# Attention and FFN on one core: scores from parts for three more pairs of batch two, their normalising on GpSimd, new prices in the order's planner

## The chip, the cores and the metric

The kernel runs on one core of a Trainium2 chip. The metric is the device time in microseconds of one execution; lower is better.

## What is computed

Causal attention for 4 batches of 12 heads, 448 positions and 64 dimensions, then a layer norm and a two-layer FFN (768 to 3072 to 768) with a residual. All arrays are float32 to the caller.

```python
scores = scale * np.matmul(q, k.transpose(0, 1, 3, 2))      # causal mask, softmax over k
x = np.matmul(attn, v)                                      # heads side by side: 4 x 448 x 768
xn = (x - mu) / np.sqrt(var + 1e-06) * g_ln
out = x + np.maximum(xn @ w_ch1, 0.0) @ w_ch2
```

## The kernel before

**Tiles and stages.** Heads go in pairs, six to a batch; a pair fills the 128 partitions with two times 64 dimensions. Batches are counted from 0 here, so that "batch two" of the title is batch index 1. Batch 0's attention runs first; the attention of batch index 1 runs beside the FFN of batch index 0, and so on. The FFNs of batch indexes 2 and 3 run together at the end as a `Pair`, with seven products of halves in place of eight. FFN weights are split into two parts of type F32R, high and low, and an FFN matmul has three products (`wh xh`, `wh xl`, `wl xh`) of 448 columns each. Tiles named `ph`, `po`, `bX`, `bY`, `bA` are its results.

**Scores of a pair, two ways.** `both` (L868) takes q and k as loaded, in F32, and issues the matmuls of the two heads side by side, each on 64 of the array's rows (operand `first_qk` for batch 0, `qkraw` for batch index 1), in three groups of the four row blocks: `[3], [0, 2], [1]`. `scores` (L893) uses all 128 rows: `split1` and `split2` (L839, L848) first make `qs` (q above, its rounding rest below), `kh` and `kl` (the parts of k), and two matmuls of type F32R add up in one bank. `BOTH` (L66) names the batches that go by `both` beside batch 0. A row block i has 112 (i + 1) columns: 112, 224, 336, 448. `least` then masks and takes the running minimum on DVE, `exps` the exponential on ACT, `norm` (L934) multiplies each row block by the reciprocal sum: on GpSimd for batch 0, on DVE or ACT for the others. `transposes` (L963) turn the blocks on TensorE (results `pt`), `pv` (L986) multiplies by the values: eight matmuls on 64 columns each side, results `px`, 16 records in the profile. `TWOS` (L77) lists pairs whose value matmuls are issued together with the next pair's.

**Layer norm.** `mean` (L1041) sums over partitions with a matmul of ones; `squares` (L1069) ends with the column `ve` = 1/sigma; `spread` (L1094) and, for the last two batches, `banks` (L1239) turn it to rows with four transposes (`rb`), and `apply1` scales the input of the FFN.

**Order of the work.** Nothing is issued directly. `Plan` records every instruction as a task with the time by which it is needed, `cost` (L300) gives each a duration, and `run` (L419) goes through a list schedule of the five queues (TensorE, GpSimd, DVE, ACT and SP, which issues all DMAs). `t.mode` is TensorE's form: "" for the whole array, "rows" for matmuls on 64 rows, "columns" for those on 64 columns. A change of form costs `CHANGE` in the plan, and work of the present form goes first unless other work is due `TOGETHER` earlier (L486 to L492). Where `either` gives several engines for a task, the schedule chooses. `MOVES` shifts due times of some tasks by drawn amounts, `STARTS` gives the slots at which pairs start. The resulting order is fixed in the program; on the chip, semaphores do the waiting.

Of the kernel before, what the change touches and what calls it, by code (L numbers as in the profile page):

```python
# [11 lines left out]
F32 = mybir.dt.float32  # L12
# [11 lines left out]
P = 128  # L24
# [17 lines left out]
SECOND = 16000  # L42
BEHIND = 12000
EARLY_SLOT = 1450
SLACK, DMA_SLACK = 154, 5280
CHANGE, TOGETHER = {'': 0, 'columns': 100, 'rows': 188}, 13200
# [12 lines left out]
BOTH, RAT = (1,), [0, 0, 0]  # L59
SAT, TAT, NAT, END = [0, 0, 1, 1, 2], [4, 5, 5, 6, 6], [3, 3], 7  # L60
EV1, EV = [1, 1, 1, 1, 1], [1, 1, 0, 1, 0]
STARTS = {
    0: [-1, 6, 12, 18, 24, 30],
    1: [0, 5, 10, 14, 19, 24],
    2: [30, 34, 38, 42, 46, 50],
    3: [54, 58, 62, 66, 70, 74],  # L66
# [4 lines left out]
TWOS = {3: [0, 2, 4]}  # L71
VAR0, RB0, XC, XG = 1, 5, 3, 3
SPLIT = (1, 2, 3)
COPIED = [NP, NP, 3, 0]
AHEAD0 = 4
WARM, FILL, HOLD = 10, 29160, 4000
# [7 lines left out]
NDVE = 7  # L84
# [12 lines left out]
class View:  # L97
# [44 lines left out]
    def to_broadcast(self, shape):  # L142
        return self._new(self.p, self.idx, lambda t: t.to_broadcast(shape))

# [55 lines left out]
class Plan:  # L200
# [99 lines left out]
    def cost(self, t):  # L300
# [3 lines left out]
        if t.engine == "sync":  # L304
            x = (t.outs + t.ins)[0]
            rate = 360 if x.p[1] - x.p[0] == P else 240 if x.p[1] - x.p[0] == D else 150 if n == 512 else 330
            cost = 650 if x.buf.name == "first_qk" else 60
            return cost, (x.p[1] - x.p[0]) * n * 4 * 320 / rate, False
        if t.engine == "tensor":
            if t.kw.get("rhs") is not None and t.kw["rhs"].dtype == BF16:  # L310
                return 0.84 * n, 220, False
            if t.method == "transpose":
                return 97 if t.ins[0].dtype == F32 else 80, 220, False
# [93 lines left out]
    @staticmethod  # L407
    def drawn(n, seed):
# [10 lines left out]
    def run(self, need, hint):  # L419
# [9 lines left out]
        tiled = {"": [], "rows": [], "columns": []}  # L429
# [26 lines left out]
        while True:  # L456
# [28 lines left out]
            elif e == "tensor":  # L485
# [3 lines left out]
                heap = min((h for h in tiled.values() if h), key=lambda h: h[0])  # L489
                same = tiled[mode]  # L490
                if same and same[0][0] < heap[0][0] + TOGETHER:
                    heap = same  # L492
# [103 lines left out]
def kernel(ctx, tc, qk, v, w1, w2, g, out):  # L596
# [172 lines left out]
    class Att:  # L769
        count = {"nm": 0, "PT": 0}  # L770

        def __init__(self, b):
            self.b, self.twos = b, TWOS.get(b, [])
            self.t = {}
            self.turn = 0
            self.done = set()
# [35 lines left out]
        def load(self, p):  # L812
# [4 lines left out]
            elif self.b in BOTH:  # L817
# [8 lines left out]
        def load_v(self, p):  # L826
# [3 lines left out]
            else:  # L830
                pool = probs if p - 1 in self.twos else ap
                vt = pool.tile([C, 2, NC, D], F32, tag="v", name="vt", bufs=1)
# [101 lines left out]
        def norm(self, p, h):  # L934
# [6 lines left out]
            eng = nc.vector if self.b or p >= NDVE else nc.gpsimd  # L941
            for i in (0, 1, 3, 2):
# [4 lines left out]
                if eng is nc.gpsimd:  # L947
# [719 lines left out]
```

## Time and profile before

| | us |
|---|---|
| three runs | 792.99, 793.04, 793.08 |
| median | 793.04 |
| the profiled execution's own time | 792.73 |
| its span, first to last instruction | 790.7 |
| PE busy in the span | 783.6 |
| DVE, ACT, POOL busy | 665.8, 519.0, 303.0 |

The span is cut into pieces by engine and line. PE is TensorE's matmul row, PEld its weight load. Matmuls are pipelined, so the duration of one is longer than its distance to the next; distances are read from starts. The granted clock is 0.999 of full speed over the span, which is the level of 2.4 GHz. Every instruction that the plan issues carries the same line, L587, so work is told apart by tile names. The chain in order of time lists what released what, with runs of alike instructions as one piece; its pieces follow one another, so their lengths add up to the time.

### The profile page before, as it was taken

To read this page: it belongs to the slowest core of one execution; us is meant where nothing else is said; L and a number is where in the kernel's file an instruction comes from. 1 tells how busy PE (TensorE), PEld (TensorE's weight loads), DVE (VectorE), ACT (ScalarE), POOL (GpSimd) and SP (SyncE) were. 2 spreads that over 40 slices of the span, in tenths; PEclk is the share of its full clock that TensorE was granted. 3 is DMA by queue.
4 is the path that set the end of the run, shared out by engine and by line. 5 is a ranking of instruction groups with operands and counts; after the bars stand their busy time and mean duration, and the time that the engine had idled before them with its cause. 6 is when DMAs were issued, how large, how long until landed. Compare 5 with 4: busy or idle time off the path is not lost.

```text
span 790.7 us, 13663 instructions
## 1 busy us (share of the span) xinstructions
PE 783.6 (99%) x4554; PEld 720.0 (91%) x4554; DVE 665.8 (84%) x1406; ACT 519.0 (66%) x1155; POOL 303.0 (38%) x306
## 2 busy tenths in 40 slices
PE   9999999999999999999999999999999999999998
PEld 4679888888899989999898899999999999999998
DVE  6899998989999998888887479887887878888785
ACT  6999978888999775766755255664545546455461
POOL 4645000001262262242111168655546464464540
PEclk9999999999999999999999999999999999999999
DMA  9788889677778878778886765335253342523434
GB/s 212 269 255 289 319 308 349 209 295 249 303 250 310 303 277 286 249 270 278 249 311 204 251 193 173 112 92 168 62 161 102 107 130 78 157 90 115 126 94 167
DMA packets 62470, 166.50 MB, mean 211 GB/s; under 512 B 7136, under 2 KB 27744, under 8 KB 62400
## 3 DMA queue, kind: packets, MB, share of 16 engines
q1 hardware_dynamic: 62400, 165.63, 63.3%
q8 instruction: 36, 0.59, 0.3%
q14 instruction: 34, 0.28, 0.1%
HBM read 116.62 MB, written 39.94 MB: 198 GB/s over the span
## 4 chain that ended last, share of the span: by engine, by line
PE 92%; ACT 4%; DVE 2%; DMA 1%; issue 0%; POOL 0%; SPq 0%; ACTq 0%; POOLq 0%; DVEq 0%
PE po L587 21%; PE bX L587 21%; PE ph L587 18%; PE bY L587 10%; PE sc L587 6%; PE bA L587 5%; PE px L587 5%; PE pt L587 5%; ACT P L587 1%; ACT bits L587 1%; DVE P L587 0%; DMA scratch<-w 0%; DMA first_qk<-qk_dram 0%; DVE wl L587 0%; DVE w L587 0%; ACT wh L587 0%
## 5 line engine op out<-in xcount | busy, mean ns | idle before, releaser
L587 ACT ACTIVATE P<-P,least 112x336 f32<-112x336 f32 (+3 forms) x176 | 91.2, 522 | 26.4 <-DVE least L587 25.9
L587 PE MATMUL ph<-xh,wh 128*128 128x450 f32 (+1 forms) x288 | 104.4, 364 | 0.2 <-DVE hl L587 0.2
L587 PE MATMUL po<-hh,wh 128*128 128x448 f32 x288 | 103.9, 361 | 0.0
L587 PE MATMUL ph<-xh,wl 128*128 128x450 f32 (+1 forms) x288 | 102.8, 359 | 0.0
L587 PE MATMUL po<-hl,wh 128*128 128x448 f32 x288 | 102.8, 357 | 0.0
L587 PE MATMUL ph<-xl,wh 128*128 128x450 f32 (+1 forms) x288 | 102.8, 358 | 0.0
L587 PE MATMUL po<-hh,wl 128*128 128x448 f32 x288 | 102.5, 356 | 0.0
L587 ACT ACTIVATE wp<-s 128x256 fp32r<-128x256 f32 (+1 forms) x114 | 51.6, 461 | 58.1 <-PE bX L587 16.4
L587 DVE CUSTOM_DVE_ANT_0 P<-sc,mask 112x224 f32<-112x224 f32 (+3 forms) x176 | 71.5, 441 | 13.7 <-PE sc L587 12.2
L587 POOL TENSOR_TENSOR s<-u 128x256 f32<-128x256 f32 (+1 forms) x60 | 55.3, 937 | 68.2 <-DMA u<-scratch 48.7
L587 ACT ACTIVATE wk<-u 128x256 fp32r<-128x256 f32 (+1 forms) x89 | 41.1, 464 | 54.3 <-PE bX L587 36.1
L587 DVE TENSOR_TENSOR wp<-s,wp 128x256 fp32r<-128x256 f32 (+1 forms) x120 | 68.6, 582 | 3.1 <-ACT wp L587 2.8
L587 POOL TENSOR_TENSOR h<-b,h 128x448 fp32r<-128x448 f32 x36 | 43.2, 1201 | 52.5 <-ACT h L587 31.9
L587 POOL TENSOR_TENSOR kl<-qkraw,kh 128x896 fp32r<-128x896 f32 x12 | 28.7, 2392 | 86.8 <-ACT kh L587 42.7
L587 POOL TENSOR_TENSOR acc<-acc,xT 128x448 f32<-128x448 f32 x12 | 15.5, 1291 | 118.4 <-DVE xT L587 98.1
L587 ACT ACTIVATE PT<-pt 112x448 f32<-112x448 f32 x88 | 45.8, 540 | 22.7 <-PE pt L587 21.1
L587 PEld LDWEIGHTS ph<-xh,wh 128*128 128x128 f32 x288 | 54.4, 189 | 2.7 <-issue 1.7
L587 DVE TENSOR_TENSOR xT<-xT,bX 128x448 f32<-128x448 f32 x72 | 44.5, 618 | 14.3 <-PE bX L587 14.2
L587 PEld LDWEIGHTS ph<-xl,wh 128*128 128x128 f32 x288 | 54.5, 189 | 2.1 <-issue 1.7
L587 PEld LDWEIGHTS po<-hl,wh 128*128 128x128 f32 x288 | 54.6, 189 | 1.5 <-issue 1.1
L587 PEld LDWEIGHTS ph<-xh,wl 128*128 128x128 f32 x288 | 54.4, 189 | 1.5 <-DVE xl L587 0.5
L587 PEld LDWEIGHTS po<-hh,wl 128*128 128x128 f32 x288 | 54.5, 189 | 0.7 <-issue 0.5
(193 smaller groups left out, 2174.8 us busy)
## 6 DMA issues: line engine op xcount, KB each, us to landing
raw<-w_dram SPq DMA_DIRECT2D x39, 768.0 KB, 6.7
scratch<-w SPq DMA_DIRECT2D x48, 384.0 KB, 4.7
full<-scratch SPq DMA_DIRECT2D x24, 768.0 KB, 6.9
kept<-wl SPq DMA_DIRECT2D x30, 384.0 KB, 5.8
qkraw<-qk_dram SPq DMA_DIRECT2D x12, 896.0 KB, 5.5
u<-scratch SPq DMA_DIRECT2D x24, 384.0 KB, 3.8
u<-scratch SPq DMA_DIRECT2D x36, 256.0 KB, 2.9
PR<-P SPq DMA_DIRECT2D x18, 490.0 KB, 6.5
```

The lines of the kernel that those rows point to most:

```text
L587: getattr(getattr(nc, t.engine), method)(*args, **kw)
```

## The change

- `BOTH` becomes a list of pairs for each batch: of batch index 1, pairs 0, 1 and 2 stay with `both`; pairs 3, 4 and 5 go by `split1`, `split2` and `scores`.
- `NORMS` sets the engine of `norm` for each pair: P is GpSimd, E is DVE or ACT. Batch index 1's pairs 1 to 5 go to GpSimd.
- `TWOS` adds pair 4 of batch index 2, whose value matmuls are issued with pair 5's.
- `SENT`: 1/sigma of batch index 2 is written to a row in memory and read back broadcast, in place of four transposes. `WIDE`: in `spread` of batch index 1 the mean is copied to a PSUM bank.
- `mean` stores the two parts with even and odd elements apart and reads them woven, as the FFN does, and both matmuls depend on both parts.
- The last addition of the pair's FFN and its store are cut into two halves.
- In the planner: transposes have a form of their own ("turned"), prices of changes are 10, 178 and 192 ns, the preference for the present form is 70 times the price of the change, `SLACK`, `SECOND`, `HOLD`, `MOVES`, `SAT` and two `STARTS` have other values.

```diff
-SECOND = 16000
+SECOND = 32000
-SLACK, DMA_SLACK = 154, 5280
-CHANGE, TOGETHER = {'': 0, 'columns': 100, 'rows': 188}, 13200
+SLACK, DMA_SLACK = 192, 5280
+CHANGE, NEAR, TOGETHER = {'': 0, 'turned': 10, 'columns': 178, 'rows': 192}, 192, 70
...
 MOVES = [
-    (305651422, 1000, 256, 16860, 90000), (1865966318, 1000, 128, -20100, 79900),
-    (1507149061, 3000, 128, 242781, 302781), (1428196934, 3000, 32, 161652, 221652),
-    (690608532, 20000, 32, 389252, 399252), (1144641184, 8000, 16, 48048, 58048),
-    (637256214, 20000, 16, 259121, 279121), (1540864739, 8000, 16, 268427, 278427),
-    (635955765, 3000, 256, 110408, 120408),
+    (305651422, 1000, 256, 16860, 90000), (1507149061, 3000, 128, 242781, 302781),
+    (1428196934, 3000, 32, 161652, 221652), (637256214, 20000, 16, 259121, 279121),
+    (1073982846, 1000, 64, -6297, 53703), (475912916, 20000, 16, 212061, 232061),
+    (272716789, 1000, 32, 168281, 228281), (1922429363, 8000, 32, 353206, 363206),
 ]
...
-BOTH, RAT = (1,), [0, 0, 0]
-SAT, TAT, NAT, END = [0, 0, 1, 1, 2], [4, 5, 5, 6, 6], [3, 3], 7
+BOTH, RAT = {1: [0, 1, 2], 2: [], 3: []}, [0, 0, 0]
+SAT, TAT, NAT, END = [0, 0, 1, 0, 2], [4, 5, 5, 6, 6], [3, 3], 7
...
 STARTS = {
-    0: [-1, 6, 12, 18, 24, 30],
+    0: [-1, 6, 12, 17, 24, 30],
     1: [0, 5, 10, 14, 19, 24],
     2: [30, 34, 38, 42, 46, 50],
-    3: [54, 58, 62, 66, 70, 74],
+    3: [54, 58, 62, 67, 70, 74],
 }
...
-TWOS = {3: [0, 2, 4]}
+TWOS = {2: [4], 3: [0, 2, 4]}
...
-SPLIT = (1, 2, 3)
+SPLIT, SENT, WIDE = (1, 2, 3), (2,), ('mb',)
...
-WARM, FILL, HOLD = 10, 29160, 4000
+WARM, FILL, HOLD = 10, 29160, 3200
...
-NDVE = 7
+NORMS = ['PPPPPP', 'EPPPPP', 'EEEEEE', 'EEEEEE']
...
+
+    def turned(self, f):
+        return self._new(self.p, self.idx, f)
...
+            if x.buf.name.startswith("row"):
+                return 60, 1000 * 320, False
             return cost, (x.p[1] - x.p[0]) * n * 4 * 320 / rate, False
...
             if t.method == "transpose":
-                return 97 if t.ins[0].dtype == F32 else 80, 220, False
+                t.mode = "turned"
+                return 97 if t.ins[0].dtype == F32 else 78, 220, False
...
     @staticmethod
+    def changed(old, new):
+        if old == new:
+            return 0
+        return NEAR if {old, new} == {"rows", "columns"} else max(CHANGE[old], CHANGE[new])
+
...
-        tiled = {"": [], "rows": [], "columns": []}
+        tiled = {x: [] for x in CHANGE}
...
                 while heap:
                     x = heapq.heappop(heap)
                     heapq.heappush(tiled[tasks[x[1]].mode], x)
-                heap = min((h for h in tiled.values() if h), key=lambda h: h[0])
-                same = tiled[mode]
-                if same and same[0][0] < heap[0][0] + TOGETHER:
-                    heap = same
+                heap = min(
+                    (h[0][0] + TOGETHER * self.changed(mode, x), h[0][1], x) for x, h in tiled.items() if h
+                )
+                heap = tiled[heap[2]]
...
-            elif self.b in BOTH:
+            elif p in BOTH[self.b]:
...
-            eng = nc.vector if self.b or p >= NDVE else nc.gpsimd
+            way = NORMS[self.b][p]
             for i in (0, 1, 3, 2):
                 pp = self.t["P", p, h][:, OFF[i]:OFF[i + 1]]
                 kw = dict(
                     out=pp, in0=pp, scalar1=r[:, i // 3, i % 3:i % 3 + 1], scalar2=1.0, op0=ALU.mult, op1=ALU.mult,
                 )
-                if eng is nc.gpsimd:
-                    eng.tensor_scalar(**kw)
-                else:
-                    nc.either(
-                        ("vector", "tensor_scalar", (), kw),
-                        ("scalar", "activation", (), dict(
-                            out=pp, in_=pp, func=ACTF.Copy, scale=r[:, i // 3, i % 3:i % 3 + 1],
-                        )),
-                    )
+                ways = [
+                    ("gpsimd", "tensor_scalar", (), kw),
+                    ("vector", "tensor_scalar", (), kw),
+                    ("scalar", "activation", (), dict(
+                        out=pp, in_=pp, func=ACTF.Copy, scale=r[:, i // 3, i % 3:i % 3 + 1],
+                    )),
+                ]
+                nc.either(*[ways[x] for x in {"P": (0,), "E": (1, 2), "A": (0, 1, 2)}[way]])
 
...
             mb = ps.tile([P, S], F32, tag="sc", name="mb", bufs=2)
             if self.b in SPLIT:
                 hi, lo = (ap.tile([P, S], F32R, tag="PT", name="acc" + x, bufs=8) for x in "hl")
-                move(hi, self.acc)
-                lows = dict(out=lo, in0=self.acc, in1=hi.bitcast(F32), op=ALU.subtract)
+                move(halves(hi), apart(self.acc))
+                lows = dict(
+                    out=halves(lo), in0=apart(self.acc), in1=halves(hi).bitcast(F32), op=ALU.subtract
+                )
                 nc.either(("gpsimd", "tensor_tensor", (), lows), ("vector", "tensor_tensor", (), lows))
+                last = [n for n, w, _ in lo.buf.log if w]
                 for x, t in enumerate((hi, lo)):
-                    nc.tensor.matmul(mb, lhsT=ones.to_broadcast([P, P]), rhs=t, start=(x == 0), stop=(x == 1))
+                    nc.record("tensor", "matmul", (mb,), dict(
+                        lhsT=ones.to_broadcast([P, P]), rhs=woven(t), start=(x == 0), stop=(x == 1),
+                    )).deps.update(last)
             else:
                 nc.tensor.matmul(
                     mb, lhsT=ones.bitcast(F32).to_broadcast([P, P]), rhs=self.acc, start=True, stop=True
@@ -1086,13 +1109,28 @@
...
+            if self.b in SENT:
+                self.row = dr.tile([1, S], F32, name=f"row{self.b}")
+                nc.sync.dma_start(out=self.row.turned(lambda t: t.rearrange("o (i c) -> c (o i)", c=C)), in_=ve)
+
+        def sigma(self, tag, bufs):
+            t = ap.tile([P, S], F32, tag=tag, name="rbs", bufs=bufs)
+            nc.sync.dma_start(out=t, in_=self.row.turned(lambda t: t.broadcast_to([P, S])))
+            return t
 
         def over_sigma(self):
+            if self.b in SENT:
+                self.rb = self.sigma("rb", 1)
+                return
             self.rb = ap.tile([P, S], F32, tag="rb", name="rbs", bufs=1)
             move(self.rb, self.spread_one(self.t["ve"]))
 
         def spread(self):
-            self.t["mb"], self.t["rb"] = self.kept, self.spread_one(self.t["ve"])
+            self.t["mb"] = self.kept
+            self.t["rb"] = self.sigma("PT", 8) if self.b in SENT else self.spread_one(self.t["ve"])
+            for x in WIDE:
+                src, self.t[x] = self.t[x], ps.tile([P, S], F32, tag="sc", name=x, bufs=2)
+                move(self.t[x], src)
             self.parts()
             self.xg = [ap.tile([P, S], F32, tag="PT", name="xg", bufs=8) for _ in range(XG)]
...
-                if self.b and self.b not in BOTH:
+                both = self.b == 0 or p in BOTH[self.b]
+                if not both:
                     put(pre, t0 - (2 if self.b == 1 else 1), self.split1, p)
                     put(pre, t0 - 1, self.split2, p)
...
-                for x, grp in enumerate([] if self.b and self.b not in BOTH else RGROUPS if p or self.b else FIRSTS):
+                for x, grp in enumerate([] if not both else RGROUPS if p or self.b else FIRSTS):
...
-                for x, grp in enumerate(SGROUPS if self.b and self.b not in BOTH else []):
+                for x, grp in enumerate([] if both else SGROUPS):
                     put(post, t0 + sat[x], self.scores, p, grp)
...
             for a in self.at:
                 a.t["rb"] = rb = ps.tile([P, S], F32, tag="pt", name="rb", bufs=2)
-                for x in range(NC):
+                if a.b in SENT:
+                    move(rb, a.sigma("PT", 8))
+                for x in range(NC) if a.b not in SENT else ():
                     nc.tensor.transpose(
                         rb[:, x * C:(x + 1) * C], a.t["ve"][:, x:x + 1].to_broadcast([C, P]), ident[:C, :C]
                     )
...
             def add(i, j, src):
                 m = 2 * blk[2] + i
                 t = self.at[j].xT[m]
-                nc.vector.tensor_tensor(out=t, in0=t, in1=src, op=ALU.add)
                 self.left[j, m] -= 1
-                if self.left[j, m] == 0:
-                    nc.sync.dma_start(out=out[self.at[j].b, m], in_=t)
+                last = (b, k) == self.items[-1]
+                for x in ((0, S // 2), (S // 2, S)) if last else ((0, S),):
+                    y = slice(*x)
+                    nc.vector.tensor_tensor(out=t[:, y], in0=t[:, y], in1=src[:, y], op=ALU.add)
+                    if self.left[j, m] == 0:
+                        nc.sync.dma_start(out=out[self.at[j].b, m][:, y], in_=t[:, y])
```

## Rows read from the trace of the kernel before

**Rows 1.** Of the page: busy time of TensorE; shares of the chain that ended last.

```profile
PE 783.6 (99%) x4554; PEld 720.0 (91%) x4554; DVE 665.8 (84%) x1406; ACT 519.0 (66%) x1155; POOL 303.0 (38%) x306
...
PE 92%; ACT 4%; DVE 2%; DMA 1%; issue 0%; POOL 0%; SPq 0%; ACTq 0%; POOLq 0%; DVEq 0%
```

**Rows 2.** Busy time by stretch: start:end, us, then each engine's busy us (instructions), clock, DMA.

```profile
0.00:80.00 80.00, 76.71 (x491) 54.34 (x492) 67.57 (x206) 72.36 (x186) 41.85 (x74) 1.00 0.85 258
80.00:480.00 400.00, 399.76 (x2452) 361.64 (x2450) 348.18 (x765) 288.67 (x621) 103.08 (x71) 1.00 0.79 271
...
100.00:200.00 100.00, 100.00 (x599) 85.35 (x598) 91.11 (x211) 83.08 (x167) 6.72 (x5) 1.00 0.78 284
```

**Rows 3.** The chain in order of time, 136 to 146 us: start us, us, what.

```profile
136.65 0.94 PE sc L587 x4
137.59 2.09 PE po L587 x10
139.68 0.95 PE sc L587 x8
...
142.34 0.57 PE sc L587 x4
```

**Rows 4.** The chain in order of time, 183 to 192 us.

```profile
184.32 0.94 PE sc L587 x4
...
187.29 0.95 PE sc L587 x8
...
189.96 0.56 PE sc L587 x4
```

**Rows 5.** The chain in order of time, 291 to 303 us.

```profile
291.92 2.04 PE px L587 x16
293.95 5.30 PE ph L587 x27
299.26 0.86 PE sc L587 x6
300.12 1.13 PE ph L587 x6
301.25 0.39 PE sc L587 x4
...
301.85 0.38 PE sc L587 x2
```

**Rows 6.** The chain in order of time, near 268 us and 378 us.

```profile
268.64 0.38 PE rb L587 x4
269.03 1.15 PE po L587 x6
...
377.96 3.92 PE px L587 x32
```

**Rows 7.** Groups of DVE, 98 to 200 us; then tiles r, qs, kl: duration ns min/median/max.

```profile
L587 DVE TENSOR_SCALAR P<-P,r 112x448 f32<-112x448 f32 (+3 forms) x27 | 8.4, 363 | 0.1
...
L587 DVE TENSOR_SCALAR P<-P,r x88: 264/386/2418, 101.5 to 426.1; 112x448 f32<-112x448 f32 x26, 112x336 f32<-112x336 f32 x23, 112x224 f32<-112x224 f32 x20, 112x112 f32<-112x112 f32 x19
...
L587 POOL TENSOR_SCALAR P<-P,r x32: 357/498/642, 10.4 to 43.3; 112x112 f32<-112x112 f32 x8, 112x224 f32<-112x224 f32 x8, 112x448 f32<-112x448 f32 x8, 112x336 f32<-112x336 f32 x8
...
L587 DVE TENSOR_TENSOR qs<-qkraw,qs x12: 1089/2002/3058, 146.6 to 412.0; 64x896 fp32r<-64x896 f32 x12
...
L587 ACT ACTIVATE qs<-qkraw x10: 934/941/986, 144.7 to 408.4; 128x896 fp32r<-128x896 f32 x10
...
L587 POOL TENSOR_TENSOR kl<-qkraw,kh x12: 2135/2144/3271, 190.7 to 408.6; 128x896 fp32r<-128x896 f32 x12
```

**Rows 8.** Order of time from 786.5 us; DMA issues (KB each, us to landing); stores of out_dram.

```profile
787.14 0.62 DVE L587 TENSOR_TENSOR xT<-xT,bX 128x448 f32<-128x448 f32 x1 [0.51 <-PE bX L587]
...
wk<-kept SPq DMA_DIRECT2D x54, 128.0 KB, 2.1
...
DMA to landing us min/median/max: 1.9/2.6/10.7
```

More of the change, by code (lines that the diff above doesn't have):

```diff
@@ L407, in drawn @@
     @staticmethod
+    def changed(old, new):
+        if old == new:
+            return 0
+        return NEAR if {old, new} == {"rows", "columns"} else max(CHANGE[old], CHANGE[new])
+    @staticmethod
     def drawn(n, seed):
@@ L773, in __init__ @@
             self.b, self.twos = b, TWOS.get(b, [])
+            if b == 1 and self.twos:
+                self.more = ap.tile([P, 4 * S], F32, tag="qkraw", name="more", bufs=1)
             self.t = {}
@@ L831, in load_v @@
                 pool = probs if p - 1 in self.twos else ap
-                vt = pool.tile([C, 2, NC, D], F32, tag="v", name="vt", bufs=1)
+                if self.b == 1 and p - 1 in self.twos:
+                    vt = self.more[:C, 2 * S:2 * S + 2 * NC * D].rearrange("p (h j d) -> p h j d", h=2, j=NC)
+                else:
+                    vt = pool.tile([C, 2, NC, D], F32, tag="v", name="vt", bufs=1)
             nc.sync.dma_start(out=vt, in_=v[self.b, p])
@@ L968, in transposes @@
                 self.count["PT"] += 1
-            t = ap.tile([C, S], F32, tag=tag, name="PT", bufs=bufs)
+            if self.b == 1 and tag in ("y", "rb"):
+                t = self.more[:C, :S] if tag == "y" else self.more[:C, S:2 * S]
+            else:
+                t = ap.tile([C, S], F32, tag=tag, name="PT", bufs=bufs)
             o = 0
```

## The prediction

> **What bounds the kernel now.** I read the page first. Its busy table and its chain that ended last [rows 1] say that TensorE carries the program: PE is busy for 783.6 of 790.7 us and has 92% of the chain. A busy PE alone proves little, so I read the busy times by stretch next [rows 2]. From 80 to 480 us PE is busy for 399.76 of 400 us. Only the first 80 us have idle PE time, 3.29 us (80 less 76.71), beside the tail. In the stretch 100 to 200 us, where most of the edited work lies, DVE is busy for 91.11 us and ACT for 83.08, POOL for 6.72. Third I read the chain in order of time at the places that the diff touches [rows 3 to 6]. There the pieces follow each other on PE without a hole, so from 80 us on the time is the sum of PE's pieces, and an edit is worth what it takes from that sum. An FFN matmul counts 0.19 us (6 in 1.13 us) [rows 5].
>
> What this chain also shows is the price of a change of form. An FFN run behind a visit of score matmuls from 64 rows, or of value matmuls, is about 0.20 us longer than its count: 10 matmuls in 2.09 us instead of 1.89 [rows 3], 27 in 5.30 instead of 5.10 behind a value visit [rows 5]. So each visit that stands alone costs 0.20 us on top of its own pieces. Scores from parts don't show it: the six FFN matmuls behind them take the plain 1.13 us [rows 5].
>
> **The change part by part.**
>
> *Three pairs of batch two.* Pairs 3, 4 and 5 of batch index 1 are scored by `both` now. Pair 3 has visits of 0.94, 0.95 and 0.57 us, 2.46 us together, two of them alone (0.40 us) and the third beside a value visit [rows 3]: 2.86 us. Pair 5 has 0.94 and 0.95 on the two sides of a value visit, and 0.56 alone [rows 4]: 2.45 + 0.20 = 2.65 us. Pair 4 repeats pair 5's pattern. Sum 8.16 us. The value visit stays in both kernels and pays its own change. After the change a pair is scored as batch index 2 is: 0.86 us for a head's widths 448, 112 and 336, 0.39 us for width 224 of both heads, 0.38 for the other head's 448 [rows 5], and the other head's 112 and 336, which are 0.86 - 0.38 = 0.48. That is 2.11 us a pair, 6.33 for three. **Gain 1.8 us.** Its bounds: 1.0 if the value visits, which lose their neighbours, meet T or score visits badly (0.2 us at each of four places), 2.6 if they all find one another.
>
> Here a rule of the Trainium skill speaks against the edit. TensorEngine Tiling (Array Packing), section Theoretical Speedup, promises up to twice the speed where the contraction is 64 or less, and `both` is such a packing; leaving it should cost, and by the page the three pairs would go from 7.4 us of pieces to an estimated 14.8. The trace doesn't agree: 2.11 us against 2.45 before any change of form [rows 4, 5]. In the code the two parts are tiles of type F32R and the packed operands are F32, so the two forms are not alike but for the packing.
>
> *What feeds them.* Each of the three pairs now needs two moves, on ACT about 0.94 us each, a DVE subtraction (1.09 at the least, 2.00 at the median) and a POOL subtraction of 2.14 us [rows 7]. The load has twice the bytes of a pair's two small loads. On SP these stand in front of weight loads; the issue count falls by one a pair. All that lies beside PE. Its cover is ACT's 17 and DVE's 9 idle us of the stretch 100 to 200 [rows 2], and if it is gone scores come late and PE waits: the third rival.
>
> *Normalising on POOL.* In 98 to 200 us DVE gives 8.4 us to 27 such instructions [rows 7], which go, with ACT's share. POOL does one in 0.498 us at the median [rows 7], so a pair of 2 heads by 4 takes 4.0 us on an engine that has 93 us free. The wait that this adds is for POOL: transposes of a pair now wait behind its queue, where kl and the running sum stand too. A pair has some 24 us to the next one's start (pairs 3 and 5 start at 136.65 and 184.32 us) [rows 3, 4], so I cost it at nothing. Bounds: 1 us of gain in the early part, where batch index 1's pair 1 leaves ACT and DVE, and the loss of the third rival.
>
> *One more shared value visit.* A value visit alone takes 2.04 + 0.20 us [rows 5], two together 3.92 [rows 6] + 0.20. 4.48 - 4.12 = 0.36; I take **0.3**, since one of batch index 2's two last visits stood beside score pieces already and may lose a neighbour. Bounds 0 and 0.36.
>
> *Sigma of batch index 2 through memory.* Four transposes go: 0.38 us and 0.02 us of the run behind them (6 matmuls in 1.15 us instead of 1.13) [rows 6]. **Gain 0.4.** In their place stand two DMAs and one PSUM fill on ACT or DVE, with a whole batch's FFN between them and their reader; cover is ample. A load that the trace doesn't show, 4-byte pieces to a row, can take several times the 2.1 us of a plain small one [rows 8] before it matters. The copy of the mean to PSUM for batch index 1 is one ACT or DVE instruction, takes a second SBUF operand from six DVE instructions, and holds the second of the two score banks until the sixth is done; scores of batch index 2 queue behind that, PE goes on with FFN matmuls (six follow the rb transposes at once) [rows 6]: zero.
>
> *Prices of the plan.* Transposes get a mode with 10 ns a change. The row confirms the size: 0.02 us behind a visit [rows 6]. Bunching can save only that on each visit; I take **0.1**, bounds 0 and 0.6. The other prices hardly change a choice (13200 before, 12460 to 13440 now). New seeds and starts redraw the whole order; I take zero and carry +-1.6 us, half of PE's idle 3.29 us at the start [rows 2]. The woven mean takes the same two matmuls: zero, bounds +-0.3.
>
> *The tail.* The last addition ends at 787.14 + 0.62 = 787.76 us [rows 8], 2.94 us before the end of the span, and its store of 224 KB lands in 2.6 us. With halves, the second ends some 0.1 us later (a second fixed part) and moves 112 KB, near the 2.1 us of a 128 KB load [rows 8]. **Gain 0.2**, bounds +0.2 lost and 0.5 gained.
>
> Sum: 1.8 + 0.3 + 0.4 + 0.1 + 0.2 = 2.8 us. The profiled execution took 792.73 us, 0.31 under the median of 793.04. 792.73 - 2.8 = 789.9, and with 0.31 the forecast is **790.2 us**. A measurement of this kernel can tell about 0.2% from no change, which is 1.6 us: faster is below 791.4, slower above 794.6.
>
> **The rivals.**
>
> 1. *The start closes as well.* ACT is busy for 72.4 and DVE for 67.6 of the first 80 us, and PE idles there [rows 2]; with a pair's normalising gone to POOL, half or all of the 3.29 us can go. 790.2 - 1.6 = 788.6, at most 786.9. Against it: batch index 0 normalised on POOL before, so only one pair is relieved there.
>
> 2. *The gain is given back in small waits.* From 80 us on PE had 0.24 us of idle time in 400 [rows 2]; a redrawn order can hardly be better and can be worse. Each of the three pairs has a new late comer, kl on POOL, 2.14 us [rows 7] behind that engine's normalising. If each is late by 0.9 us, 2.7 us come back: 792.9 us. For it speaks that such a subtraction took up to 3.27 us [rows 7]; against it, that batch index 2 lives with the same chain and no idle PE.
>
> 3. *DVE becomes the bound in 100 to 200 us (slower).* POOL gets 4 pairs by 8 by 0.498 = 15.9 us and 3 by 2.14 = 6.4, 22.3 us in all, and where POOL works DVE stretches: the qs subtraction takes from 1.09 to 3.06 us, normalising up to 2.42 where its minimum is 0.26 [rows 7]. DVE has 8.9 us idle, wins 8.4 and gets 3.3 to 6.0 for qs: 11.3 to 14 us of room. So it decides from the point where more than half of POOL's time stands in DVE's way. At three quarters, 16.7 - 11.3 = 5.4 us fall on PE: 795.6; at all of it 801. Against it: POOL waits for DVE as often as DVE for POOL, and hl, which PE waits for, reads PSUM. SBUF — State Buffer of the Trainium skill, section Who interferes with whom, says that the pair of ports is locked for a whole instruction and the other engine blocks; the stretched rows agree, and by that rule the lock time would be this rival's 22.3 us.
>
> 4. *Packing is worth twice.* If the unpacked scores were at half the packed rate, three pairs would cost 3 x (4.9 - 2.7) = 6.6 us more instead of 1.8 less: 798.6. The rows of batch index 2 show the contrary [rows 5]. (It is the rule of the Trainium skill's Tiling page above, told as a mechanism of this kernel.)
>
> That the change doesn't do what it says could only touch the shared visit (0.3 us), inside the forecast.
>
> **How the numbers follow.** The forecast has 0.56, with its own range 788.7 to 791.4 from the bounds above. Rival 1 has 0.15, rival 2 0.16, rival 3 0.12, rival 4 0.01. Faster is forecast and rival 1, 0.71; same is rival 2, 0.16; slower is rivals 3 and 4, 0.13. The range reaches from 787.4, inside rival 1, to 793.9, above rival 2, and leaves out rivals 3 and 4 and the far end of 1.
>
> **What would show it.** Right: PE's score matmuls from qkraw halve and those from kh and kl rise by a quarter; the chain at the three pairs has no FFN run lengthened by 0.20 us behind scores; one more value visit of x32; 12 rb transposes in place of 16; PE idle from 80 to 480 us stays under 1 us. Wrong: PE idle time with a DVE or POOL releaser in 100 to 200 us, DVE at 98% there with longer wl and w instructions, POOL kl as releaser of sc, or a first 80 us that is longer than now.

## The result and the profile after

The changed kernel takes **798.64 us** (median of 6 runs, 795.66 to 801.71) against 793.01 us (6 runs, 792.58 to 794.29): a ratio of 1.007, with a 95% interval of 1.0047 to 1.0093. It is slower by 5.6 us, where 2.8 us less were forecast, and lies above the forecast range. The profiled execution took 799.22 us with a span of 797.4 us.

The page of the kernel after: its busy table, its DMA count, and the first row of its chain that ended last:

```profile
PE 785.5 (99%) x4550; PEld 726.9 (91%) x4550; DVE 660.7 (83%) x1380; ACT 523.4 (66%) x1152; POOL 339.6 (43%) x350
...
DMA packets 62791, 168.11 MB, mean 211 GB/s; under 512 B 7584, under 2 KB 27680, under 8 KB 62720
...
PE 83%; DVE 8%; ACT 3%; POOL 2%; issue 2%; DMA 1%; DVEq 0%; POOLq 0%; ACTq 0%
```

PE's share of the chain fell from 92% [rows 1] to 83%, and DVE's rose from 2 to 8%: the end of the program hangs on pieces of the other engines now. Where they come in is seen in the busy times by stretch (start:end, us, then each engine's busy us, the granted clock, DMA):

```profile
0.00:80.00 80.00, 77.28 (x492) 55.17 (x493) 67.81 (x209) 74.09 (x188) 39.96 (x72) 1.00 0.85 259
80.00:480.00 400.00, 394.38 (x2412) 361.08 (x2411) 335.20 (x725) 287.57 (x611) 133.30 (x111) 0.99 0.81 272
...
100.00:200.00 100.00, 99.29 (x603) 89.52 (x602) 90.30 (x185) 86.42 (x166) 41.45 (x48) 1.00 0.82 292
...
454.00:457.00 3.00, 0.73 (x4) 0.38 (x2) 1.79 (x4) 0.60 (x2) 0.00 (x0) 1.00 1.00 342
457.00:459.00 2.00, 0.70 (x2) 0.43 (x3) 1.94 (x4) 1.63 (x3) 1.15 (x1) 0.71 0.88 363
459.00:461.00 2.00, 2.00 (x6) 1.81 (x7) 1.76 (x4) 0.28 (x1) 0.77 (x1) 0.50 0.04 15
```

From 80 to 480 us PE is idle for 5.62 us (400 less 394.38) instead of 0.24 [rows 2]. The largest piece stands at 454 to 459 us, where 1.43 of 5 us are busy. Behind it PE is busy without a hole, but at a granted clock of 0.50, the level of 1.2 GHz. PE's waits from 80 to 480 us name four releasers (us in total, times, longest):

```profile
PE mb L598 <- ACT acch L598: 2.8, 1, 2.8
PE sc L598 <- DVE xc L598: 1.2, 1, 1.2
PE mb L598 <- POOL accl L598: 0.8, 1, 0.8
PE pt L598 <- POOL P L598: 0.6, 2, 0.3
```

The place of the longest is read in order of time (start us, us, engine, what, in brackets the idle time before it and its releaser), with the issues of SP ahead of it:

```profile
439.05 0.42 SPq L598 DMA_DIRECT2D row<-ve  x1
...
447.13 0.73 SPq L598 DMA_DIRECT2D old<-kept_mean  x1
...
450.52 0.32 SPq L598 DMA_DIRECT2D rbs<-row  x1
...
455.20 0.63 DVE L598 COPY mb<-old 128x448 f32<-128x448 f32 x1 [5.35 <-DMA old<-kept_mean]
456.40 0.55 ACT L598 ACTIVATE rb<-rbs 128x448 f32<-128x448 f32 x1 [5.23 <-DVE hl L598]
456.88 0.59 ACT L598 ACTIVATE acch<-acc 128x448 fp32r<-128x448 f32 x1
457.52 0.46 PE L598 MATMUL mb<-acch,ones 128*128 128x448 f32 x1 [2.79 <-ACT acch L598]
...
459.29 0.58 PE L598 MATMUL ph<-xl,wh 128*128 128x448 f32 x1
459.66 0.58 PE L598 MATMUL ph<-xh,wl 128*128 128x448 f32 x1
```

This is what sending sigma through memory left behind. The two fills, `mb<-old` on DVE and `rb<-rbs` on ACT, stand in their engines' queues and wait 5.35 and 5.23 us. (The bracket of the second names `hl` on DVE, which ended just then too. The load `rbs` landed 0.1 us before the fill started, and in experiments 6 and 8, where DVE was done earlier, the fill starts 0.1 us behind that landing again.) `acch`, which batch index 3's mean needs on PE, comes after the fill on ACT although its own input was done. The FFN matmuls behind the pause start 0.37 us apart instead of 0.19. The DMA issues say what the fills wait for (KB each, us from issue to landing):

```profile
old<-kept_mean SPq DMA_DIRECT2D x1, 224.0 KB, 8.1
...
rbs<-row SPq DMA_DIRECT2D x1, 224.0 KB, 5.8
row<-ve SPq DMA_DIRECT2D x1, 1.8 KB, 11.4
```

The row of 1.8 KB is written as 448 pieces of 4 bytes. (The page has 7584 packets under 512 B. It has 7104 in experiment 2, where sigma goes by transposes, and 7248 in experiment 8, where the same row goes in 112 pieces: 336 fewer, which is 448 less 112.) It takes 11.4 us, and `old`, issued 8 us behind it, lands in 8.1 us; before, the same load took 5.7. The next four transfers that SP issued land in the order of their issue and all behind the write: the write at 450.5 us, then 451.5, 453.9, 455.2 (`old`) and 456.3 (`rbs`). The first of the four was issued at 443.73 us and took 7.8 us; in experiment 8 it took 3.3. `rbs` reads the row, so SP issues it only when the write has landed.

**A ledger.** I added, from 80 us on, the time of each PE matmul from its start to the next one's, by kind, and set apart what exceeds the usual spacing. Scores and pairs, T and value visits (T visits are the transposes, `pt`) and rb came out 2.7 us less; 2.6 were forecast for them, 2.8 less the tail's 0.2. A few tenths of the 2.7 hang on where a wait is taken to begin. Against that stand about 9.2 us more of waits: the mean's wait 3.7, fourteen matmuls at half clock 2.6 (14 by 0.184), waits for POOL's normalising 1.6 (the table lists only pauses, this counts late starts too), for a score bank that DVE's `xc` holds 1.35. 9.2 - 2.7 = 6.5 is the distance of the two profiled executions, 799.22 - 792.73.

### The profile page after: what moved, and what is told of

It reads as the page before. It is cut to its first block, busy times and chain, and to the rows that moved or that the text cites. A ratio compares the mean times of both kernels' runs of the same rounds, so it can differ in the third digit from the quotient of the medians.

```text
span 797.4 us, 13700 instructions
## 1 busy us (share of the span) xinstructions
PE 785.5 (99%) x4550; PEld 726.9 (91%) x4550; DVE 660.7 (83%) x1380; ACT 523.4 (66%) x1152; POOL 339.6 (43%) x350
## 2 busy tenths in 40 slices
DMA packets 62791, 168.11 MB, mean 211 GB/s; under 512 B 7584, under 2 KB 27680, under 8 KB 62720
## 4 chain that ended last, share of the span: by engine, by line
PE 83%; DVE 8%; ACT 3%; POOL 2%; issue 2%; DMA 1%; DVEq 0%; POOLq 0%; ACTq 0%
PE bX L598 21%; PE po L598 18%; PE ph L598 15%; PE bY L598 10%; PE bA L598 5%; PE sc L598 5%; PE px L598 5%; PE pt L598 4%; DVE P L598 2%; DVE wl L598 2%; DVE w L598 1%; POOL P L598 1%; ACT P L598 1%; DMA old<-kept_mean 1%; DVE ph L598 1%
## 5 line engine op out<-in xcount | busy, mean ns | idle before, releaser
L598 POOL TENSOR_SCALAR P<-P,r 112x336 f32<-112x336 f32 (+3 forms) x72 | 43.6, 623 | 66.9 <-DVE r L598 53.8
L598 POOL TENSOR_TENSOR kl<-qkraw,kh 128x896 fp32r<-128x896 f32 x15 | 35.8, 2386 | 63.7 <-ACT kh L598 26.8
L598 PEld LDWEIGHTS po<-hh,wh 128*128 128x128 f32 x288 | 54.8, 190 | 1.1 <-issue 0.5
L598 DVE TENSOR_TENSOR wl<-w,wh 128x768 fp32r<-128x768 f32 x48 | 51.7, 1080 | 4.4 <-ACT wh L598 4.1
```

The lines of the kernel that those rows point to most:

```text
L598: getattr(getattr(nc, t.engine), method)(*args, **kw)
```

## The experiments

The theories, and the letters that some expectations use. **Q**: the order of DVE's and ACT's queues, the fill ahead of `acch`, makes the pause. **D**: the write in small pieces delays the loads behind it, and whatever waits for those is late, in any order. **C**: PE's pause lowers the granted clock, and the lower clock costs time of its own. W, in later expectations, is D told of the write's 448 pieces; P and R are explained where they first stand. Against them stood that normalising on POOL or the redrawn order carries the loss.

**1. The fill behind `acch`.** The order of after, with one ACT instruction moved:

```diff
+        line.remove(fill)
+        line.insert(line.index(acch) + 1, fill)
```

> The changed kernel with its order as it is, but for one instruction: ACT's fill of rb from the broadcast load is put behind acch, the first part of the sum for batch index 3's mean. Theory Q (ACT's queue: acch waits behind a fill whose row takes from 439.05 us, the issue of its write, to 456.4 us to come back): the 3.7 us of waits of PE at 454 to 459 us go, and with them the 14 matmuls at half the clock (14 x 0.184 = 2.6 us): 799.2 - 6.3 = 792.9 us in the profiled execution, no mb wait over 0.3 us, clock 1.00 in all stretches. Rival D (the late load of the kept mean, for which DVE waits 5.4 us, or the memory traffic as such): the mean still comes late, PE waits at least 2 us, over 797 us.

799.53 us, ratio 1.0074 (1.005 to 1.0098): no gain. In order of time:

```profile
455.40 0.35 PE L598 MATMUL mb<-acch,ones 128*128 128x448 f32 x1
...
456.67 0.63 DVE L598 COPY mb<-old 128x448 f32<-128x448 f32 x1 [5.98 <-DMA old<-kept_mean]
...
470.13 1.56 PE L598 MATMUL var<-g_sb,xc 128*112 128x1 f32 x8 [2.46 <-POOL xc L598]
```

Behind it, by stretch:

```profile
470.00:480.00 10.00, 9.87 (x40) 9.32 (x41) 3.90 (x7) 1.57 (x3) 2.34 (x3) 0.66 0.43 138
```

PE's wait for `mb` is gone, but the fill on DVE still waits for `old` (8.7 us to land), so the centred values come late and PE pauses 2.5 us at 467 us, with a granted clock of 0.66 in the 10 us from 470 on. ACT's order alone is not the cause; the late load finds another victim.

**2. Sigma by transposes again**, the rest of after kept:

```diff
-SPLIT, SENT, WIDE = (1, 2, 3), (2,), ('mb',)
+SPLIT, SENT, WIDE = (1, 2, 3), (), ('mb',)
```

> The changed kernel without the way through memory: 1/sigma of batch index 2 is turned by four transposes again, the numbering of the plan's tasks is kept, so that the order is the same up to 440 us. Theory Q: four transposes cost 0.4 us, the waits of 3.7 us and the half clock of 2.6 us go, less what DVE's wait for the kept mean still costs, since the plan puts acch behind it there (up to 1 us): 793.3 to 794.3 us. Rival D: with the 448 small packets gone the kept mean's load lands as before the change, in 5.7 us and not 8.1; PE's wait falls too, but by what the load is earlier (2.4 us), and 1 to 2 us of wait stay, with some matmuls at half the clock: 795 to 797 us.

793.47 us, ratio 1.0007 (0.9998 to 1.0017). That is 5.2 us under after, nearly the whole loss. The load's landing:

```profile
old<-kept_mean SPq DMA_DIRECT2D x1, 224.0 KB, 2.5
```

PE's waits from 80 us on:

```profile
PE sc L598 <- DVE xc L598: 1.2, 1, 1.2
PE pt L598 <- POOL P L598: 0.6, 2, 0.3
```

`old` lands in 2.5 us in place of 8.1, and the waits for the mean are gone. Two small ones stay.

**3. PE's wait filled** with 20 matmuls that nobody reads, ahead of the mean's first matmul; nothing else differs from after:

```diff
+            for _ in range(20 if n == self.filled else 0):
+                nc.tensor.matmul(real(t.outs[0]), lhsT=..., rhs=..., start=True, stop=True)
```

> The changed kernel in its own order, with 20 bf16 matmuls of 448 columns on the bank of the mean put in front of the first mb matmul, which overwrites them: PE has work in the wait and the mean comes as late as it did. Theory C (the clock falls because PE idles): the 20 take about 3.8 us where PE waited 2.8, the granted clock stays at 1.00 and the matmuls behind go at 0.19 us: 799.2 - 2.6 + up to 1.0 = 796.6 to 797.6 us. If the half clock comes from something else (the load on the chip, the time in the program), it stays, and the time is 799.2 to 800.2 us.

797.82 us (4 runs), ratio 1.0065 (1.0048 to 1.0082); the profiled execution took 796.0. Busy times by stretch, after first:

```profile
459.00:464.00 5.00, 5.00 (x14) 4.51 (x15) 3.40 (x8) 1.47 (x3) 3.21 (x3) 0.50 0.02 6
```

and with the wait filled:

```profile
459.00:464.00 5.00, 5.00 (x28) 5.00 (x27) 4.95 (x10) 3.26 (x6) 3.80 (x4) 1.00 0.36 105
```

The same 5 us hold 28 matmuls at clock 1.00 instead of 14 at 0.50. `acch` is ready no sooner than in after, and the first matmul of the mean even starts 0.9 us later, behind the added ones; only PE's idleness was taken away, and the lower clock went with it. In the profiled executions that gave 3.2 us; the medians, with few runs, differ by 0.8 us, and their intervals overlap.

**4. Normalising on DVE and ACT again**, the rest of after, sigma through memory too:

```diff
-NORMS = ['PPPPPP', 'EPPPPP', 'EEEEEE', 'EEEEEE']
+NORMS = ['PPPPPP', 'EEEEEE', 'EEEEEE', 'EEEEEE']
```

> The changed kernel with the normalising of batch index 1 on DVE or ACT again, as before the change; the plan is made anew with the same seeds. Theory P (the transposes wait behind POOL's normalising): the five waits of PE on POOL P from 102 to 194 us, 1.6 us together, go: 797.6 us, if the rest of the order keeps its waits. Rival R (any new order has waits of its own): the POOL waits go and others of 1 to 3 us come, at other places and behind other engines: 798 to 801 us. In both the wait at the mean near 455 us can come out otherwise, and is read apart.

796.26 us (792.85 to 798.48), ratio 1.0036 (1.0015 to 1.0057), some 2.4 us under after. By stretch:

```profile
80.00:440.00 360.00, 359.77 (x2233) 331.11 (x2232) 321.19 (x725) 278.05 (x598) 92.51 (x59) 1.00 0.83 285
440.00:480.00 40.00, 37.54 (x214) 35.16 (x213) 25.75 (x39) 14.22 (x24) 20.07 (x18) 1.00 0.64 186
```

The longest wait of PE, and the stretch behind it:

```profile
PE var L598 <- POOL xc L598: 2.5, 1, 2.5
...
464.00:467.00 3.00, 0.54 (x5) 0.25 (x3) 1.96 (x2) 1.05 (x2) 2.07 (x2) 1.00 0.90 312
467.00:470.00 3.00, 3.00 (x22) 2.95 (x22) 0.72 (x2) 0.00 (x0) 1.02 (x1) 1.00 0.91 277
```

Up to 440 us PE has 0.23 us of idle time, so the waits for POOL and for the score bank are gone with the normalising and the order drawn for it. What stays is the pause behind the late `old` (6.9 us here). In this execution, of 793.94 us, the clock is 1.00 behind that pause of 2.5 us, where experiment 1 had 0.66 behind one as long; the four executions at a mean clock of 0.998 or less took 795.95 to 798.48 us.

**5. Sigma through memory alone**, put into the kernel before:

```diff
+                if a.b == 2:
+                    row = dr.tile([1, S], F32, name="row2")
+                    nc.sync.dma_start(out=row.turned(...), in_=a.t["ve"])
+                    nc.sync.dma_start(out=t, in_=row.turned(lambda t: t.broadcast_to([P, S])))
+                    move(rb, t)
```

> The kernel before with nothing but batch index 2's 1/sigma sent through memory (write of the row, broadcast load and PSUM fill in place of four transposes); the plan puts the write in front of the kept mean's load there too, acch on DVE ahead of everything, and the mean's fill on ACT. Theory W (the write of 448 pieces of 4 bytes takes 11 us and the loads behind it land late, so that whatever fill stands in an engine's queue blocks that queue): the kept mean's load takes 7 to 9 us instead of 5.7, ACT's fills of mb and rb block hh and the squares, PE waits 2 to 4 us near 455 to 470 us and may fall to half the clock: 795 to 799 us. Theory Q alone (only acch behind the rb fill counts): acch is ahead here, so four transposes less give 792.5 us.

794.88 us (10 runs, 792.55 to 797.5), ratio 1.0022 (1.0005 to 1.0038). Landings:

```profile
old<-kept_mean SPq DMA_DIRECT2D x1, 224.0 KB, 10.0
...
row<-ve SPq DMA_DIRECT2D x1, 1.8 KB, 11.9
```

PE's longest wait is 1.1 us, for `xc` on DVE. The slow write comes with the part and not with the order of after; how much it costs depends on who waits for `old`, here 1.6 us. That is just under theory W's range; theory Q alone, 792.5 us, does not hold.

**6. The row written early**, issued at 351.98 us in place of 439.05, the order of after otherwise; and **7. the same without POOL's normalising** (the edit of 4):

```diff
+        line.remove(write)
+        line.insert(ve + 1, write)
```

> The changed kernel in its own order, but for one DMA: the write of the row is issued right behind the instruction that makes 1/sigma, near 350 us, instead of near 439 us. Theory W: the kept mean's load lands in about 2.5 us, as without the write, SP no longer waits for the write before it issues the broadcast load, the fills come in time, and PE's waits at 454 to 459 us and the half clock go: 792.5 to 793.5 us, 0.4 us below the kernel with transposes at best. Rival (the broadcast load of 5.8 us, or the order of the fills, is late by itself): acch still stands behind the rb fill, PE still waits 1 us or more near 455 us, 794.5 us or more.

> The changed kernel with batch index 1's normalising on DVE or ACT and the row written early: both suspected losses away, the rest of the change kept. Theories W and P: against the profile of the kernel with the normalising alone put back (793.9 us with 2.3 us of PE waiting for POOL's xc and none for POOL's P) the 2.3 us go: 791.0 to 791.9 us, faster than the kernel before by 0.1 to 0.25%. Rival R (a new order has its own waits in any case): 793 us or more, with waits at new places.

796.16 us, ratio 1.004 (1.0026 to 1.0054), and 795.87 us, ratio 1.0037 (1.0023 to 1.0051). Landings of the first:

```profile
old<-kept_mean SPq DMA_DIRECT2D x1, 224.0 KB, 2.4
...
row<-ve SPq DMA_DIRECT2D x1, 1.8 KB, 7.4
```

PE's waits in it, but for those for `xc` and for `P` on POOL, which are as in after:

```profile
PE pt L598 <- DMA PR<-P: 1.0, 1, 1.0
PE mb L598 <- POOL accl L598: 0.8, 1, 0.8
PE mb L598 <- ACT acch L598: 0.7, 1, 0.7
```

`old` is quick again, but the write now stands ahead of the loads `PR<-P`, and PE waits for one of them at 370 us: 1.0 us in the first, 2.7 in the second. Moving the write moves the damage. The other two waits are the rival of the first expectation: `acch` still stands behind the fill of `rb`, which waits for its load until 456.0 us, and the mean is 1.5 us late. In the second, whose newly drawn order doesn't have `acch` behind the fill, that wait is gone.

**8. The row in pieces of 16 bytes.** The same 1.8 KB, laid out so that each of the 112 partitions writes its four numbers in one piece; the fill puts them in order. The order of after:

```diff
-... out=self.row.turned(lambda t: t.rearrange("o (i c) -> c (o i)", c=C)), in_=ve)
+... out=self.row.turned(lambda t: t.rearrange("o (c i) -> c (o i)", c=C)), in_=ve)
```

> The changed kernel in its own order, with the row laid out so that each of 112 partitions writes one piece of 16 bytes in place of four of 4 bytes; the PSUM fill reads it reordered. Theory W in its narrow form (the number of small pieces makes the write slow): the write lands in 5 to 7 us instead of 11.4, the kept mean's load in 3 to 5, PE waits under 1 us near 455 us, no half clock: 792.5 to 794 us. Wide form (any write and read through memory there stands behind the bulk loads): the write takes 8 us or more, PE waits 2 us or more: 796 to 799 us.

795.02 us, ratio 1.0028 (1.0015 to 1.0042), 3.6 us under after. Landings:

```profile
old<-kept_mean SPq DMA_DIRECT2D x1, 224.0 KB, 2.4
...
row<-ve SPq DMA_DIRECT2D x1, 1.8 KB, 4.3
```

The fill of `rb` in order of time:

```profile
453.77 0.99 ACT L598 ACTIVATE rb<-rbs 128x448 f32<-128x448 f32 x1 [2.63 <-DMA rbs<-row]
```

A quarter of the pieces: the write lands in 4.3 us instead of 11.4, at the same place in SP's order, and `old` in 2.4 instead of 8.1; the clock stays at 1.00. So the number of pieces was most of the matter, 3.6 us of it. The result lies between the ranges of the two forms of the expectation, because PE still waits 1.4 us for the mean (0.6 for `acch`, 0.8 for `accl`): the fill waits for the broadcast load, and `acch` stands behind it. The Trainium skill, DMA: Bandwidth & Descriptors, section Specifications, gives 512 B as the least transfer for line rate; both layouts are under it, so that sentence alone doesn't tell these two runs apart.

**9. The pairs from parts alone**, in the kernel before, with its old prices:

```diff
-BOTH, RAT = (1,), [0, 0, 0]
+BOTH, RAT = {1: [0, 1, 2], 2: [], 3: []}, [0, 0, 0]
```

> The kernel before with nothing but the three pairs of batch index 1 scored from parts (plan made anew, normalising on DVE and ACT, old prices and seeds). Forecast of the term: 1.8 us less of PE's pieces; score matmuls and the FFN runs behind them give it in the trace. Theory R (a new order brings its waits): up to 1.5 us of it is lost again in waits of PE from 80 to 480 us: 791.2 to 792.7 us. Rival: DVE and ACT don't hold the extra moves, waits of over 2 us, at or above 793 us.

794.81 us, ratio 1.0023 (1.0012 to 1.0034): slower, a miss of mine. By stretch:

```profile
100.00:200.00 100.00, 100.00 (x611) 90.99 (x610) 95.18 (x212) 89.27 (x176) 14.67 (x8) 1.00 0.83 300
200.00:300.00 100.00, 98.34 (x604) 89.62 (x603) 94.91 (x199) 87.15 (x182) 44.37 (x30) 1.00 0.83 287
```

The longest wait of PE:

```profile
PE sc L587 <- DVE xg L587: 0.7, 1, 0.7
```

Where the pairs are, from 100 to 200 us, PE has no idle time: the form itself costs no wait there, and it gains. From the start of the 150th FFN matmul to that of the 750th, with the same other matmuls between them, it is 164.2 us here (85.32 to 249.48) and 166.2 before (83.98 to 250.19), 2.0 us less. But up to the 1050th, at 336 us, 3.0 us are given back: 1.66 of them are idle time from 200 to 300 us, at visits that wait for DVE, the rest stands in longer pieces of the order drawn for it. This execution, the slowest of its seven, also lost 1.3 us ahead of the 150th and some 1.1 behind 400 us, which I can't assign.

**10. The tail in halves alone**, in the kernel before:

```diff
+                for x in ((0, S // 2), (S // 2, S)) if last else ((0, S),):
+                    y = slice(*x)
+                    nc.vector.tensor_tensor(out=t[:, y], in0=t[:, y], in1=src[:, y], op=ALU.add)
+                    if self.left[j, m] == 0:
+                        nc.sync.dma_start(out=out[self.at[j].b, m][:, y], in_=t[:, y])
```

> The kernel before with the last addition and its store in halves and nothing else; the order is the same up to the last two instructions. Forecast of the term: 0.2 us less (bounds 0.5 less, 0.2 more): 792.7 us against 792.9.

793.18 us, ratio 0.9995 (0.9986 to 1.0005): not told from zero. From the start of the last additions to the end of the span it is 3.48 us instead of 3.56 (790.70 - 787.14 [rows 8]).

**11. Both suspects back**: sigma by transposes and normalising on DVE and ACT (the edits of 2 and 4). The pairs, the shared value visit, the prices, the woven mean and the tail stay. **12. Normalising back, the row in 16 bytes** (the edits of 4 and 8). The first:

```diff
-SPLIT, SENT, WIDE = (1, 2, 3), (2,), ('mb',)
+SPLIT, SENT, WIDE = (1, 2, 3), (), ('mb',)
-NORMS = ['PPPPPP', 'EPPPPP', 'EEEEEE', 'EEEEEE']
+NORMS = ['PPPPPP', 'EEEEEE', 'EEEEEE', 'EEEEEE']
```

> The changed kernel with the two suspected losses undone: batch index 1's normalising on DVE or ACT, batch index 2's 1/sigma by transposes; three pairs from parts, the shared value visit, the halved tail and the planner's prices stay. By the profile with the normalising alone put back, the FFN was 2.1 us ahead of the kernel before at 398 us. Theories W and P: that stays to the end, 790.6 to 791.4 us. Rival R (new waits at the mean or elsewhere eat it): 792.4 us or more.

> As the last one, but with 1/sigma through memory in 16-byte pieces in place of the transposes. If the number of pieces was the matter, it gains the 0.4 us of the transposes: 790.2 to 791.2 us. If the way through memory itself blocks DVE or ACT, PE waits near 455 us and some executions fall to half the clock: 793 to 797 us.

791.71 us, ratio 0.998 (0.9971 to 0.999), and 791.88 us, ratio 0.9987 (0.9978 to 0.9996): both beat the kernel before and the kernel after. By stretch, of the first:

```profile
80.00:480.00 400.00, 399.62 (x2459) 368.75 (x2458) 350.20 (x769) 293.11 (x623) 116.83 (x80) 1.00 0.80 275
...
100.00:200.00 100.00, 100.00 (x613) 91.59 (x612) 96.19 (x217) 89.83 (x180) 14.61 (x8) 1.00 0.82 295
```

PE's idle time from 80 to 480 us is 0.38 us, and DVE at 96% in 100 to 200 us holds nobody up. In the second the row is written in 3.0 us and `acch` doesn't stand behind the fill, and the loss through memory is gone; but the 0.4 us that the way through memory was to gain doesn't show either (791.88 against 791.71 us, where the expectation had 790.2 to 791.2).

## Why the prediction was wrong

**Sigma through memory is the step that failed.** "Gain 0.4 ... cover is ample" looked for cover of the two DMAs' own reader and bounded a slow write by that reader. That cover was not there: 1/sigma is ready at 351.3 us, but the plan issues the write only at 439.05, when the reader, the fill of `rb`, is 12 us away (456.40 - 5.23 = 451.2); write and broadcast load together took 17.2 us, to 456.3. And it didn't look at the transfers issued behind the write on the same queue. DVE was ready for `old` 2.7 us after its issue (455.20 - 5.35 - 447.13), so a load that takes 8.1 had no cover. With transposes instead the kernel is 5.2 us faster (798.64 - 793.47): the step cost 5.2 us where it was to give 0.4. In the ledger the direct waits are 3.7 and the half clock 2.6 us. That the way through memory causes it is shown by experiments 2 and 5, that 3.6 us of it hang on the number of pieces by experiment 8, that the lower clock followed from the pause by experiment 3. The rest, 1.4 us in experiment 8, is a wait that the sum left out as well: `rb` is filled by an engine whose queue holds `acch` behind the fill. Neither mended alone is enough (experiments 1 and 8); with both, in experiment 12, nothing is lost. The copy of the mean for batch index 1, for which the prediction says "PE goes on with FFN matmuls", cost nothing: it stands at 269 us, and PE has no wait there.

**Normalising on POOL "at nothing"** failed too, at a smaller size: 1.6 us of late transposes in the ledger. Between experiments 2 and 11, which differ in it and in the order drawn for it, the ratio falls by 0.0027, 2.1 us. The prediction had 93 us free on POOL and 24 us to the next pair, but the transposes of the same pair wait for each tile, and the engine is not as quick as assumed. Groups of after, 98 to 215 us for POOL and 98 to 200 us for DVE (busy us, mean ns of one, idle before):

```profile
L598 POOL TENSOR_SCALAR P<-P,r 112x448 f32<-112x448 f32 x10 | 11.1, 1106 | 0.0
L598 POOL TENSOR_SCALAR P<-P,r 112x336 f32<-112x336 f32 x10 | 7.9, 787 | 3.0 <-DVE r L598 3.0
...
L598 DVE TENSOR_TENSOR wl<-w,wh 128x768 fp32r<-128x768 f32 x22 | 24.6, 1117 | 1.4 <-ACT wh L598 1.1
```

The widest tile takes 1106 ns here, where batch index 0's took 636 ns in the same kernel, and DVE's `wl` went from 950 to 1117 ns. A pair's eight tiles take 5.7 us, not 4.0. So rival 3's mechanism, the two engines standing in each other's way, is in the trace: from 98 to 200 us the `wl` that share over 30% of their time with POOL's work take 1281 ns in the mean, the others 953. But what PE waited for was POOL and not DVE, which is busy for 90.30 us in 100 to 200, less than before. Nor is the longer `wl` the mark of the normalising alone, since in experiment 11, without it, the mean is 1094 ns. That the rival's 795.6 us lay on the right side of the forecast was luck. The Trainium skill, SBUF — State Buffer, section Who interferes with whom, says that a DVE instruction with two SBUF inputs, as `wl` is, contends with a GpSimd instruction that reads SBUF; the longer times on both engines agree.

**The savings were right.** After's score matmuls from `kh` and `kl` are 120 each instead of 96, those of `qkraw` 48 instead of 96, and the FFN runs behind the new score visits keep their plain length. The chain of after, in order of time:

```profile
137.99 0.48 PE sc L598 x4
138.47 7.19 PE po L598 x38
```

38 matmuls in 7.19 us are 0.189 each, without the 0.20 us that stood there before [rows 3]. A value visit of x32 more is in the chain, 12 rb transposes stand in place of 16, and the ledger gives 2.7 us where 2.6 were forecast. By experiment 9's count the pairs alone gave 2.0 us against 1.8. The prediction's test, PE's idle time under 1 us from 80 to 480 us, is what told at once that something else was wrong.

**The redrawn order at zero, +-1.6 us**, was right in its bounds, but for experiment 9, and it lost where it did anything: 1.35 us behind `xc` in after, 3.0 us in experiment 9, 1.66 of them idle, and nearly no idle time in 11. Rival 2, the gain given back in small waits, is what is left once sigma is out: 793.47 us in experiment 2 against the rival's 792.9, though the late comers are POOL's normalising and `xc`, not `kl`. The tail gave 0.08 us of the forecast 0.2. Rival 1's start closed by 0.6 us (2.72 us idle in place of 3.29 [rows 2]). Rival 4, packing worth twice, named 798.6 us, the time that came, by luck: PE's score pieces exclude it, and in experiment 11 the unpacked pairs stand and the kernel is faster than before.

Experiment 11 took 1.55 us off the kernel before, where the prediction without its sigma term would have 2.4. Counted as in the ledger its FFN matmuls take 2.9 us less than before and its scores 1.4 less, but its value visits 1.0 and its transposes 2.2 more, so the missing 0.85 can't be put down to one kind. The planner's new prices, the shared visit and the woven mean were not tried by themselves, and why the order of experiment 9 waits for DVE stays open.

## What to carry to other kernels

Before a small transfer is put into a queue, count its pieces and list the next loads behind it with the time that their readers leave them: the cost lies with them as well as with its own reader. And look up in the plan when that transfer is issued: here it left 88 us after its data were ready. A fill that waits for a DMA on DVE or ACT made everything behind it in that queue wait (5.35 and 5.23 us here), so an instruction that feeds TensorE should stand ahead of it; that alone gained nothing in experiment 1, as long as the load stayed late. And where TensorE is busy for 99% of the span, price a pause of some microseconds above its own length: 2.6 us of matmuls at the lower clock came behind 3.7 us of waits in after, though none behind 2.5 us in the profile of experiment 4.

## What was not expected of the hardware

A write of 1.8 KB in 448 pieces took 7.4 to 11.9 us to land in every run that had it, longer than the 224 KB loads issued behind it on SP. Behind the write the load of `old` took up to 10.0 us; in the five runs without such a write, 2.5 (experiment 2) to 6.1 (experiment 9). In 112 pieces the write took 3.0 to 4.3 us. Waits of 3.7 us in PE's work were followed by 14 matmuls 0.37 us apart, the level of 1.2 GHz, and matmuls whose results nobody reads kept the granted clock at 1.00. Behind pauses of 2.5 to 2.7 us it came out both ways: 1.00 in experiment 4, 0.66 in experiment 1, and 0.50 from 375 to 378 us in experiment 7. The kernel's own spread also grew: 6.0 us between the lowest and the highest of six runs of after, 1.5 us in ten of experiment 11. The clock has a part in that: of experiment 5's ten executions those at a mean clock of 1.000 took 792.6 to 794.2 us, and those at 0.998 or less 795.5 to 797.5.
